# Row sums of the key softmax moved from a reduction on VectorE to a DMA transpose and products with a mask

## The chip, the cores and the metric

The kernel runs on one core of a Trainium2 chip. The time is the device time of one execution in microseconds. The engines are named as in the profile: PE (TensorE, matrix products), PEld (its weight loads), DVE (VectorE), ACT (ScalarE), POOL (GpSimd) and SP (SyncE, which here only issues DMAs). Each engine works through its own list of instructions in order and waits where it needs another's result. PSUM, where PE writes, has eight banks.

## The reference

Two independent halves are computed and set side by side in the output of shape (1, 2048, 896).

Half A is linear attention with softmax feature maps, 16 heads of 28 columns:

```python
qkv = (x @ wqkv).reshape(B, S, 3, H, Dh)            # x: 2048 x 448
pk = einsum("bhsd,hdf->bhsf", k, w_phi)             # pq likewise from q
phi_k = concatenate([softmax(pk), softmax(-pk)])    # over the 28 columns of a head
kv = einsum("bhsf,bhsd->bhfd", phi_k, v);  z = einsum("bhsf->bhf", phi_k)
o = (phi_q . kv) / (phi_q . z + 1e-6);     a = o @ wo
```

Half B is a long convolution with a state-space kernel, 448 channels with 256 states each, over 2048 positions, plus a direct term:

```python
P = exp(dt * A * l)                                 # per channel, state and position l
K = real(einsum("dn,dnl,dn->dl", C, P, dt * B))     # the kernel of each channel
y = irfft(rfft(pad(u)) * rfft(pad(K)))[:2048] + u * Dskip
```

## The kernel before

Everything works on tensors cut to 128 partitions. The SBUF is one large buffer in which the code places its tiles by hand (`sb(offset, shape)`), and PSUM is one tensor of eight banks. Each operation of the program is not issued where it is written: it is added to a list (`prog.add`), and at the end the list is issued in the order written out in `ORDER`; which banks an operation uses is written out in `SLOTS`, one entry for each `prog.take`. Nearly every instruction therefore has the line of a helper in the profile: L198 is every product, L208 a transpose on PE, L159 every DVE operation on two tensors, L171 a multiply by a number, L184 a reciprocal, L187 an activation function, L190 a copy on ACT, L213 every DMA. L592, the reduction of the key side, has a line of its own.

Half A. x is loaded in four blocks and transposed on PE (`flip_x`); w_phi is folded into the q and k weights (`fold_weights`), so that one product gives pk. The key side (`key_side`, L578 to L618) runs over 16 tiles of 128 positions. Each tile has two groups of four products of 448 columns (pk into bank b4, v into bank b5), two exponentials on ACT from pk with signs + and - into EK (128 x 2 x 448), a copy of v on ACT, the sums of EK over each head's 28 columns on DVE (`tensor_reduce`, 2 x 16 sums in f32), their reciprocal, a multiply of v (with a column of ones added) by the reciprocals into VR (128 x 2 x 29 x 16), and eight products of EK with VR that add up over all tiles in banks bK. Tiles alternate between two buffers each of EK, V, sums, reciprocals and VR. After the last tile the sums are masked by head, transposed and multiplied by wo into M. The query side (`query_side`) runs over four blocks of 512 positions.

Half B. The channels are cut into four quarters (qt). For each, sines (`rotations`) and exponentials (`dampings`) on ACT make tables which DVE multiplies together (`damp`, `far`, `hi_tables`), PE multiplies the tables into values of K at 640 positions (`build_k`), and DMAs through DRAM re-order them (`scatter_k`). `kernel_spectrum_pair` and `kernel_spectrum` transform K with products by Fourier tables (`load_f`), `signal_spectrum` does so with u early on and stores the result in DRAM (SUd), and `conv` loads it, multiplies the spectra on DVE, transforms back on PE and adds u * DSK.

Position 0 of K is not among the 640 positions. Before, a product with a matrix of ones (L349) sums the states for each channel, and L353 adds that sum to DSK on DVE, so that the direct term carries it.

Operations on two PSUM banks at once (`two`, `args`) read both with one stride; in the old `SLOTS` such pairs can lie apart, for example "07" or "26".

Of the kernel before, what the change touches and what calls it, by code (L numbers as in the profile page):

```python
# [10 lines left out]
F32 = mybir.dt.float32  # L11
# [5 lines left out]
D_MODEL = 448  # L17
# [29 lines left out]
def _dft_tables():  # L47
# [30 lines left out]
    return tuple(_round_bf16(t) for t in (G, GI, FT, pid, hm))  # L78
# [24 lines left out]
def kernel(  # L103
# [20 lines left out]
    G_d, GI_d, F_d, P_d, M_d = (nc.inline_tensor(t, name=f"const{i}").ap() for i, t in enumerate(consts))  # L124
# [96 lines left out]
    HM = sb(3200, [112, 4, D_HEAD + 1])  # L221
    bias_hp = sb(3440, [128, 1], F32)
# [122 lines left out]
    ones = sb(212544, [128, 128])  # L345
    mset(ones, 1.0)
    dma("G", DSK, bass.AP(tensor=B_Dskip.tensor, offset=B_Dskip.offset, ap=[[0, 128], [1, D_MODEL]]))
# [5 lines left out]
    add(DSK, DSK, psum[:, bs[0], 0:D_MODEL])  # L353
# [72 lines left out]
    dma("G", HM, M_d)  # L426
    dma("G", wo, A_wo.rearrange("(c p) n -> p c n", p=112))
    V_ = [sb(181504 + 928 * i, [128, D_HEAD + 1, 16]) for i in range(2)]
    for v in V_:
        mset(v[:, D_HEAD, :], 1.0)  # L430
# [147 lines left out]
    def key_side():  # L578
        bK = prog.take("P", 6), prog.take("P", 7)
        for tn in range(16):  # L580
            ts_ = slice(128 * tn, 128 * tn + 128)
            i2 = tn % 2
            (b4,), (b5,) = prog.take("P", 4), prog.take("P", 5)
            mms(acc(psum[:, b4, 0:D_MODEL], [(xT[:, dj, ts_], Wp[1][:, dj, :]) for dj in range(4)]))
            mms(acc(psum[:, b5, 0:D_MODEL], [(xT[:, dj, ts_], WV[:, dj, :]) for dj in range(4)]))
            EK = sb(177920 + 1792 * i2, [128, 2, D_MODEL])
# [3 lines left out]
            acopy(V[:, 0:D_HEAD, :], psum[:, b5, 0:D_MODEL].rearrange("p (h d) -> p d h", d=D_HEAD))  # L590
            zk = sb(187072 + 128 * i2, [128, 2, 16], F32)
            prog.add("V", lambda zk=zk, EK=EK: nc.vector.tensor_reduce(  # L592
                zk, EK.rearrange("p s (h f) -> p s h f", f=D_HEAD), axis=AX.X, op=ALU.add))
            rk = sb(187328 + 64 * i2, [128, 2, 16])
            recip(rk, zk)
            VR = sb(183360 + 1856 * i2, [128, 2, D_HEAD + 1, 16])
            mul(VR, V.unsqueeze(1).to_broadcast([128, 2, D_HEAD + 1, 16]),
                rk.unsqueeze(2).to_broadcast([128, 2, D_HEAD + 1, 16]))
            mms([(psum[0:112, bK[s][0], 116 * c:116 * c + 116].rearrange("p (d h) -> p d h", h=4),
                  EK[:, s, 112 * c:112 * c + 112], VR[:, s, :, 4 * c:4 * c + 4],  # L600
                  dict(start=(tn == 0 and c == 0), stop=(tn == 15), skip_group_check=True))
                 for s in range(2) for c in range(4)])
# [81 lines left out]
    def spectrum_terms(o, ft, b, rhs, sk0, m, cp):  # L684
        n = len(TERMS[b])
        items = [(o, ft[:, cp, fi, :], rhs(kt), dict(start=(k == 0), stop=(b == 0 and k == n - 1)))
                 for k, (fi, kt) in enumerate(TERMS[b])]
        if b == 1:
            items.append((o, (NEG, ident)[cp], sk0(1 - cp, m), dict(start=False, stop=True)))
        return items  # L690

    def kernel_spectrum_pair():
        tiles = {}

        def spec(m, b):
            (bk,) = prog.take("P", 4 + b)
            items = []
            for cp in range(2):
                items += spectrum_terms(
                    view(psum[:, bk, QC * cp:QC * cp + 1], [112, 2], [1, 112]), tiles[m], b,  # L700
                    lambda kt: view(KT[0][:, kt, 0:1], [672, 2], [1, 112]),
                    lambda c, k: view(SK[0][:, 0, c, k // 4, k % 4, 0:1], [3584, 2], [1, 112]), m, cp)
# [10 lines left out]
    def kernel_spectrum(qt, tiles, banks):  # L713
        sk = SK[qt % 2]
        for m in range(0, 8, 2):
            for b in range(2):
                (bk,) = prog.take("P", banks[b])
                items = []
                for cp in range(2):
                    for k in range(2):  # L720
                        at = 112 * (2 * cp + k)
                        items += spectrum_terms(
                            psum[:, bk, at:at + 112], tiles[m + k], b, lambda kt: KT[qt % 2][:, kt, :],
                            lambda c, i: sk[:, 0, c, i // 4, i % 4, :], m + k, cp)
# [187 lines left out]
```

## Time and profile before

| | |
|---|---|
| Median of 3 runs | 332.09 us (331.78 to 334.99) |
| The profiled execution's own time | 335.36 us |
| Its span, first to last instruction | 333.4 us |
| Instructions | 8578 |
| Busy: PE, DVE, ACT | 249.7, 267.5, 205.6 us |
| Mean granted PE clock | 0.887 |
| DMA, mean | 107 GB/s |

The span is the time from the first to the last instruction of one profiled execution. Busy time is the time in which an engine has an instruction under way; a product's end is modelled, so a busy PE need not run at its peak. The granted clock is the share of full speed that PE was allowed in a stretch. The chain of waits is found backwards from the last instruction: at each step it goes to what released it, or to the instruction before it on the same engine.

### The profile page before, as it was taken

To read this page: it belongs to the slowest core of one execution; us is meant where nothing else is said; L and a number is where in the kernel's file an instruction comes from. 1 tells how busy PE (TensorE), PEld (TensorE's weight loads), DVE (VectorE), ACT (ScalarE), POOL (GpSimd) and SP (SyncE) were. 2 spreads that over 40 slices of the span, in tenths; PEclk is the share of its full clock that TensorE was granted. 3 is DMA by queue.
4 is the path that set the end of the run, shared out by engine and by line. 5 is a ranking of instruction groups with operands and counts; after the bars stand their busy time and mean duration, and the time that the engine had idled before them with its cause. 6 is when DMAs were issued, how large, how long until landed. Compare 5 with 4: busy or idle time off the path is not lost.

```text
span 333.4 us, 8578 instructions
## 1 busy us (share of the span) xinstructions
PE 249.7 (75%) x3741; PEld 186.4 (56%) x3741; DVE 267.5 (80%) x325; ACT 205.6 (62%) x340; POOL 15.6 (5%) x31
## 2 busy tenths in 40 slices
PE   2846698896699857787967577997995608979595
PEld 2735444454355544564543375647785608879595
DVE  4286958891899988696987887999996799989990
ACT  4889548887877784866847866696544421424231
POOL 7310000000000000000010000000000000100000
PEclk9975769999999985699978989999996967979899
DMA  7999105330200000042645061787509354486022
GB/s 213 253 204 237 30 2 159 111 112 0 89 23 0 0 2 1 2 89 72 122 85 234 2 168 22 157 276 247 138 4 314 74 83 168 151 210 117 0 57 58
DMA packets 51341, 35.73 MB, mean 107 GB/s; under 512 B 32008, under 2 KB 47384, under 8 KB 50920
## 3 DMA queue, kind: packets, MB, share of 16 engines
q1 hardware_dynamic: 48328, 27.90, 34.1%
q0 software_dynamic: 2976, 7.28, 7.1%
q8 instruction: 29, 0.48, 0.6%
q14 instruction: 8, 0.07, 0.1%
HBM read 26.30 MB, written 8.85 MB: 105 GB/s over the span
## 4 chain that ended last, share of the span: by engine, by line
PE 37%; DVE 28%; DMA 15%; ACT 13%; issue 4%; SPq 2%; DVEq 0%; ACTq 0%
PE psum L198 36%; DVE sbuf L159 22%; ACT sbuf L187 7%; DMA sbuf<-in_A_x_dram 5%; DMA sbuf<-in_B_C_re_dram 4%; ACT sbuf L190 4%; DMA sbuf<-SCd 4%; DVE sbuf L592 4%; SPq L213 2%; DVE sbuf L184 1%; DMA sbuf<-const 1%; ACT L187 1%; DMA SCd<-sbuf 1%; PE psum L208 0%; DVE sbuf L177 0%
## 5 line engine op out<-in xcount | busy, mean ns | idle before, releaser
L198 PE MATMUL psum<-sbuf 128*16 128x48 bf16 (+10 forms) x3632 | 237.7, 265 | 63.3 <-ACT sbuf L187 21.5
L159 DVE TENSOR_TENSOR sbuf<-sbuf 128x896 bf16<-128x896 bf16 (+13 forms) x235 | 219.5, 975 | 32.9 <-ACT sbuf L187 16.3
L198 PEld LDWEIGHTS <-sbuf 128*16 128x16 bf16 (+4 forms) x3632 | 175.3, 112 | 125.9 <-issue 70.4
L190 ACT CAST sbuf<-psum 128x448 bf16<-128x448 f32 (+4 forms) x140 | 75.4, 570 | 77.3 <-PE psum L198 70.1
L187 ACT ACTIVATE sbuf<-psum 128x448 bf16<-128x448 f32 (+4 forms) x140 | 83.9, 659 | 33.0 <-PE psum L198 31.7
L208 PE MATMUL psum<-sbuf 128*112 128x128 bf16 (+3 forms) x109 | 13.0, 305 | 16.4 <-DMA sbuf<-in_A_x_dram 7.3
L187 ACT ACTIVATE sbuf<-psum,sbuf 128x896 bf16<-128x896 f32 (+3 forms) x28 | 21.7, 807 | 2.5 <-PE psum L198 2.1
L208 PEld LDWEIGHTS <-sbuf 128*112 128x112 bf16 (+3 forms) x109 | 11.6, 207 | 17.0 <-DMA sbuf<-in_A_x_dram 8.0
L592 DVE TENSOR_REDUCE sbuf<-sbuf 128x32 f32<-128x896 bf16 x16 | 17.2, 1080 | 1.3 <-ACT sbuf L187 1.2
L177 DVE COPY sbuf<-psum 112x1024 bf16<-112x1024 bf16 (+2 forms) x16 | 7.6, 475 | 12.8 <-PE psum L208 8.6
L187 ACT ACTIVATE sbuf<-sbuf 128x896 bf16<-128x896 bf16 (+3 forms) x13 | 11.5, 901 | 8.5 <-DVE sbuf L159 7.6
L187 ACT ACT_TABLE_LOAD x11 | 14.1, 1283 | 0.9 <-PEq L896 0.7
L171 DVE TENSOR_SCALAR sbuf<-sbuf 128x3584 bf16<-128x3584 bf16 (+4 forms) x11 | 6.7, 607 | 2.1 <-PE psum L198 1.6
L184 DVE RECIPROCAL sbuf<-sbuf 128x32 bf16<-128x32 f32 (+1 forms) x20 | 7.8, 392 | 0.6
L213 POOL DMA_DIRECT2D sbuf<-SUd x4 | 2.1, 531 | 114.2 <-DVE sbuf L159 114.2
L213 POOL DMA_DIRECT2D sbuf<-const x3 | 1.7, 569 | 114.2 <-PE psum L198 114.2
L213 POOL DMA_DIRECT2D sbuf<-in_B_u_dram x8 | 6.4, 808 | 12.2 <-PE psum L208 12.2
L159 DVE TENSOR_TENSOR sbuf<-psum,sbuf 128x128 f32<-128x128 f32 (+3 forms) x10 | 4.7, 493 | 2.0 <-ACT sbuf L187 1.3
L190 ACT COPY sbuf<-psum 112x896 bf16<-112x896 bf16 x5 | 4.3, 919 | 2.3 <-PE psum L208 2.3
L190 ACT CAST sbuf<-sbuf 128x1792 bf16<-128x1792 f32 x3 | 5.1, 1691 | 0.0
L159 DVE TENSOR_TENSOR sbuf<-sbuf,psum 112x448 bf16<-112x448 bf16 (+1 forms) x2 | 1.2, 621 | 4.3 <-issue 3.4
L174 DVE SCALAR_TENSOR_TENSOR sbuf<-sbuf 128x64 f32<-128x64 f32 (+1 forms) x6 | 3.0, 506 | 0.0
(12 smaller groups left out, 9.5 us busy)
## 6 DMA issues: line engine op xcount, KB each, us to landing
sbuf<-const SPq DMA_DIRECT2D x16, 384.0 KB, 4.2
SUd<-sbuf SPq DMA_DIRECT2D x8, 448.0 KB, 4.8
sbuf<-SCd SPq DMA_DIRECT2D x16, 224.0 KB
sbuf<-SUd POOLq DMA_DIRECT2D x4, 896.0 KB, 6.2
sbuf<-const POOLq DMA_DIRECT2D x2, 1024.0 KB, 6.0
sbuf<-in_A_x_dram SPq DMA_DIRECT2D x4, 448.0 KB, 5.1
out_dram<-sbuf SPq DMA_DIRECT2D x4, 448.0 KB
sbuf<-in_B_u_dram SPq DMA_DIRECT2D x16, 112.0 KB, 4.2
```

Of the source, the lines that this page charges most:

```text
L159: prog.add("V", lambda: nc.vector.tensor_tensor(out=o, in0=a, in1=b, op=op))
L171: prog.add("V", lambda: nc.vector.tensor_scalar_mul(o, a, s))
L174: prog.add("V", lambda: nc.vector.scalar_tensor_tensor(out=o, in0=a, scalar=s, in1=b, op0=op0, op1=op1))
L177: prog.add("V", lambda: nc.vector.tensor_copy(o, a))
L184: prog.add("V", lambda: low(lambda: nc.vector.reciprocal(o, a)))
L187: prog.add("A", lambda: nc.scalar.activation(o, a, fn, **kw))
L190: prog.add("A", lambda: nc.scalar.copy(o, a))
L198: nc.tensor.matmul(o, lhsT=l, rhs=r, **kw)
L208: nc.tensor.transpose(o, i, idn)
L213: prog.add(eng, lambda: e.dma_start(out=o, in_=i))
L592: prog.add("V", lambda zk=zk, EK=EK: nc.vector.tensor_reduce(zk, EK.rearrange("p s (h f) -> p s h f", f=D_HEAD), axis=AX.X, op=ALU.add))
```

## The change

Three things are changed together, and with them the whole of `ORDER` and `SLOTS` is written anew (1104 operations instead of 1127).

First, the key side runs over eight pairs of tiles. EK holds a pair (128 x 2 x 2 x 448). The reduction is gone: one DMA from SP transposes EK, seen as 128 x 1792, into ET, 14 blocks of 128 x 128 with the positions along the columns. For each tile of the pair seven products then take the blocks of ET as weights and a constant mask HZ (7 x 128 x 32, 1 where a row belongs to one of the 32 sums, loaded at the start) and add up 32 sums per position in a PSUM bank. One reciprocal reads the 64 sums of the pair from PSUM, and one multiply makes VR of the pair. EK, V and the reciprocals have two buffers, ET and VR one.

Second, K at position 0 becomes a term of its own. The matrix of ones holds 2^-17, its product is copied by ACT to K0 instead of added to DSK by DVE, and each spectrum of the first block of K gets, in its real part, one product more: a row block of ones with K0. DSK is loaded later.

Third, every pair of banks that one instruction reads lies in neighbouring banks in the new `SLOTS` ("12", "56", "34", "01").

```diff
@@ _dft_tables, constants @@
+    hz = np.zeros((896, 32))
+    hz[np.arange(896), np.arange(896) // D_HEAD] = 1.0
+    hz = hz.reshape(7, 128, 32).transpose(1, 0, 2)
@@ position 0 @@
-    mset(ones, 1.0)
-    dma("G", DSK, bass.AP(tensor=B_Dskip.tensor, offset=B_Dskip.offset, ap=[[0, 128], [1, D_MODEL]]))
+    mset(ones, 2.0 ** -17)
...
-    add(DSK, DSK, psum[:, bs[0], 0:D_MODEL])
+    acopy(K0, psum[:, bs[0], 0:D_MODEL])
...
     dma("G", HM, M_d)
+    dma("G", DSK, bass.AP(tensor=B_Dskip.tensor, offset=B_Dskip.offset, ap=[[0, 128], [1, D_MODEL]]))
...
+    HZ = sb(186944, [128, 7, 32])
+    dma("G", HZ, Z_d)
@@ key_side @@
-        for tn in range(16):
...
-            for s in range(2):
-                af(EK[:, s, :], psum[:, b4, 0:D_MODEL], ACT.Exp, scale=1.0 - 2.0 * s)
...
-            prog.add("V", lambda zk=zk, EK=EK: nc.vector.tensor_reduce(
-                zk, EK.rearrange("p s (h f) -> p s h f", f=D_HEAD), axis=AX.X, op=ALU.add))
-            rk = sb(187328 + 64 * i2, [128, 2, 16])
-            recip(rk, zk)
...
+        for pr in range(8):
+            i2 = pr % 2
+            EK = sb(177920 + 3584 * i2, [128, 2, 2, D_MODEL])
+            ET = sb(209216, [128, 14, 128])
+            V = V_[i2]
+            for t in range(2):
...
+                for s in range(2):
+                    af(EK[:, t, s, :], psum[:, b4, 0:D_MODEL], ACT.Exp, scale=1.0 - 2.0 * s)
+                acopy(V[:, t, 0:D_HEAD, :], psum[:, b5, 0:D_MODEL].rearrange("p (h d) -> p d h", d=D_HEAD))
+            prog.add("S", lambda ET=ET, EK=EK: nc.sync.dma_start(
+                out=ET, in_=EK.rearrange("p t s f -> p (t s f)"), transpose=True))
+            (bz,) = prog.take("P", 3)
+            mms([it for t in range(2) for it in acc(
+                psum[:, bz, 32 * t:32 * t + 32], [(ET[:, 7 * t + k, :], HZ[:, k, :]) for k in range(7)])])
+            rk = sb((187392, 138784)[i2], [128, 2, 2, 16])
+            recip(rk.rearrange("p t s h -> p (t s h)"), psum[:, bz, 0:64])
+            VR = sb(205504, [128, 2, 2, D_HEAD + 1, 16])
+            mul(VR, V.unsqueeze(2).to_broadcast([128, 2, 2, D_HEAD + 1, 16]),
+                rk.unsqueeze(3).to_broadcast([128, 2, 2, D_HEAD + 1, 16]))
...
@@ spectrum_terms @@
+        pairs = [(ft[:, cp, fi, :], rhs(kt)) for fi, kt in TERMS[b]]
         if b == 1:
-            items.append((o, (NEG, ident)[cp], sk0(1 - cp, m), dict(start=False, stop=True)))
-        return items
+            pairs.append(((NEG, ident)[cp], sk0(1 - cp, m)))
+        elif cp == 0:
+            pairs.append((W[:, 0, 31, 0:128], k0))
+        return acc(o, pairs)
@@ ORDER and SLOTS: every entry new @@
...
```

More of the change, by code (lines that the diff above doesn't have):

```diff
@@ L77, in _dft_tables @@
         hm[28 * hh:28 * hh + 28, hh, :] = 1.0
-    return tuple(_round_bf16(t) for t in (G, GI, FT, pid, hm))
+    hz = np.zeros((896, 32))
+    hz[np.arange(896), np.arange(896) // D_HEAD] = 1.0
+    hz = hz.reshape(7, 128, 32).transpose(1, 0, 2)
+    return tuple(_round_bf16(t) for t in (G, GI, FT, pid, hm, hz))
 class Prog:
@@ L123 @@
     consts = _dft_tables()
-    G_d, GI_d, F_d, P_d, M_d = (nc.inline_tensor(t, name=f"const{i}").ap() for i, t in enumerate(consts))
+    G_d, GI_d, F_d, P_d, M_d, Z_d = (nc.inline_tensor(t, name=f"const{i}").ap() for i, t in enumerate(consts))
     dram = ctx.enter_context(tc.tile_pool(name="dram", bufs=1, space=bass.MemoryType.DRAM))
@@ L221 @@
     HM = sb(3200, [112, 4, D_HEAD + 1])
+    K0 = sb(86016, [128, D_MODEL])
     bias_hp = sb(3440, [128, 1], F32)
@@ L426 @@
     dma("G", HM, M_d)
+    dma("G", DSK, bass.AP(tensor=B_Dskip.tensor, offset=B_Dskip.offset, ap=[[0, 128], [1, D_MODEL]]))
     dma("G", wo, A_wo.rearrange("(c p) n -> p c n", p=112))
-    V_ = [sb(181504 + 928 * i, [128, D_HEAD + 1, 16]) for i in range(2)]
+    V_ = [sb(o, [128, 2, D_HEAD + 1, 16]) for o in (185088, 194752)]
     for v in V_:
-        mset(v[:, D_HEAD, :], 1.0)
+        mset(v[:, :, D_HEAD, :], 1.0)
+    HZ = sb(186944, [128, 7, 32])
+    dma("G", HZ, Z_d)
     mset(W[:, 0, 31, :], 1.0)
@@ new lines, in key_side @@
+        bk_ = prog.take("P", 6, 7)
+        bK = bk_[0:1], bk_[1:2]
+        for pr in range(8):
+            i2 = pr % 2
+            EK = sb(177920 + 3584 * i2, [128, 2, 2, D_MODEL])
+            ET = sb(209216, [128, 14, 128])
+            V = V_[i2]
+            for t in range(2):
+                ts_ = slice(128 * (2 * pr + t), 128 * (2 * pr + t) + 128)
+                (b4,), (b5,) = prog.take("P", 4), prog.take("P", 5)
+                mms(acc(psum[:, b4, 0:D_MODEL], [(xT[:, dj, ts_], Wp[1][:, dj, :]) for dj in range(4)]))
+                mms(acc(psum[:, b5, 0:D_MODEL], [(xT[:, dj, ts_], WV[:, dj, :]) for dj in range(4)]))
+                for s in range(2):
[11 more added lines that the diff above has]
+                rk.unsqueeze(3).to_broadcast([128, 2, 2, D_HEAD + 1, 16]))
@@ L599, in key_side @@
             mms([(psum[0:112, bK[s][0], 116 * c:116 * c + 116].rearrange("p (d h) -> p d h", h=4),
-                  EK[:, s, 112 * c:112 * c + 112], VR[:, s, :, 4 * c:4 * c + 4],
-                  dict(start=(tn == 0 and c == 0), stop=(tn == 15), skip_group_check=True))
-                 for s in range(2) for c in range(4)])
+                  EK[:, t, s, 112 * c:112 * c + 112], VR[:, t, s, :, 4 * c:4 * c + 4],
+                  dict(start=(pr == 0 and t == 0 and c == 0), stop=(pr == 7 and t == 1), skip_group_check=True))
@@ L603, in key_side @@
+                 for t in range(2) for s in range(2) for c in range(4)])
         KVN = sb(194752, [112, 2, 4, 4, D_HEAD])
@@ L682, in load_f, with spectrum_terms @@
         return t
[L684 to L687, printed above, removed]
+    def spectrum_terms(o, ft, b, rhs, k0, sk0, m, cp):
+        pairs = [(ft[:, cp, fi, :], rhs(kt)) for fi, kt in TERMS[b]]
         if b == 1:
-            items.append((o, (NEG, ident)[cp], sk0(1 - cp, m), dict(start=False, stop=True)))
-        return items
+            pairs.append(((NEG, ident)[cp], sk0(1 - cp, m)))
+        elif cp == 0:
+            pairs.append((W[:, 0, 31, 0:128], k0))
+        return acc(o, pairs)
     def kernel_spectrum_pair():
```

17 lines of the change are left out of this document (3 added, 14 removed), and 94 rows, old and new, of tables (ORDER, SLOTS).

## The prediction

> **What bounds the kernel now.** I read the engine totals first, then cut the span into stages at the places where the chain of waits changes its colour, then the chain itself.
>
> ```profile
> span 333.4 us, 8578 instructions
> ...
> PE 249.7 (75%) x3741; PEld 186.4 (56%) x3741; DVE 267.5 (80%) x325; ACT 205.6 (62%) x340; POOL 15.6 (5%) x31
> ```
>
> DVE is the fullest engine, PE is close behind. A share of the whole span says little, so here are the stages (columns: stretch, length, busy time of PE, PEld, DVE, ACT, POOL with instruction counts, granted clock, DMA share, GB/s):
>
> ```profile
> 0.00:35.50 35.50, 19.70 (x153) 16.49 (x154) 20.27 (x21) 26.89 (x29) 11.14 (x21) 0.81 1.01 220
> 35.50:84.50 49.00, 40.41 (x255) 23.15 (x254) 34.28 (x43) 36.15 (x50) 1.20 (x4) 0.90 0.21 66
> 84.50:121.50 37.00, 31.60 (x222) 18.88 (x221) 34.88 (x41) 29.51 (x56) 0.00 (x0) 1.00 0.08 26
> 121.50:157.50 36.00, 26.25 (x581) 19.03 (x580) 27.37 (x47) 23.98 (x36) 0.00 (x0) 0.76 0.16 38
> 157.50:215.60 58.10, 44.58 (x682) 29.77 (x683) 49.08 (x55) 39.15 (x67) 1.11 (x2) 0.91 0.45 112
> 215.60:296.30 80.70, 57.64 (x1303) 49.97 (x1300) 73.46 (x90) 38.79 (x84) 2.12 (x4) 0.88 0.58 170
> 296.30:324.80 28.50, 24.96 (x464) 24.64 (x464) 28.14 (x32) 9.58 (x18) 0.00 (x0) 0.93 0.33 59
> 324.80:333.40 8.60, 4.61 (x94) 4.44 (x91) 0.00 (x0) 1.60 (x3) 0.00 (x0) 1.00 0.26 56
> ```
>
> DVE's idle time is length less busy: 15.2 us while inputs load, 14.7 up to 84.5, 2.1 in the stage to 121.5 (most of the key side), then 8.6, 9.0, 7.2 and 0.4, and 8.6 after its last instruction: 65.8 in all. From 35.5 to 324.8 it works 247.2 of 289.3 us. The chain of waits shows what the full stage is made of (start, length, what):
>
> ```profile
> 94.44 1.01 DVE sbuf L592
> 95.47 0.36 DVE sbuf L184
> 95.93 0.64 DVE sbuf L159
> 96.57 1.01 DVE sbuf L592
> ```
>
> That is one key tile: row sums (L592), reciprocal (L184), multiply (L597, through the helper L159), and the next tile 2.13 us later (96.57 - 94.44). Nothing else is waited for. At the end DVE works through without a gap, to 324.78, and 8.6 us remain after it (the last products on PE, their copies, the stores):
>
> ```profile
> 296.28 28.50 DVE L159 TENSOR_TENSOR sbuf<-sbuf 128x3584 bf16<-128x3584 bf16 x32 [0.96 <-ACT sbuf L190]
> 300.83 9.78 PE L198 MATMUL psum<-sbuf 128*128 128x112 bf16 x192 [0.16 <-DVE sbuf L159]
> ```
>
> So the time is the DVE's work, plus its 65.8 us of idle time: 267.5 + 65.8 = 333.3.
>
> **The change part by part.** The groups of instructions, by shape (busy us, mean ns of one):
>
> ```profile
> L592 DVE TENSOR_REDUCE sbuf<-sbuf 128x32 f32<-128x896 bf16 x16 | 17.2, 1080 | 1.3 <-ACT sbuf L187 1.2
> L184 DVE RECIPROCAL sbuf<-sbuf 128x32 bf16<-128x32 f32 x16 | 5.6, 352 | 0.5
> L184 DVE RECIPROCAL sbuf<-sbuf 128x64 f32<-128x64 f32 x4 | 2.2, 553 | 0.1
> L159 DVE TENSOR_TENSOR sbuf<-sbuf 128x928 bf16<-128x928 bf16 x16 | 10.3, 642 | 3.6 <-ACT sbuf L190 1.6 <-issue 0.6
> L159 DVE TENSOR_TENSOR sbuf<-sbuf 128x1792 bf16<-128x1792 bf16 x36 | 38.3, 1088 | 1.0 <-ACT sbuf L190 0.6
> L159 DVE TENSOR_TENSOR sbuf<-sbuf,psum 128x448 bf16<-128x448 bf16 x1 | 0.6, 621 | 3.4 <-issue 3.4
> ```
>
> *DVE.* Out go 16 tiles at 2.13 us = 34.1. In come, for each of 8 pairs, one reciprocal of 64 elements out of PSUM into bf16 (between 0.352 and 0.553; I take 0.45, the middle), one multiply of 1856 elements (1.088 x 1856 / 1792 = 1.13) and the 0.06 by which the step of 2.13 exceeds its three instructions (1.080 + 0.352 + 0.642 = 2.07): 1.64, eight times 13.1. The add of L353 (0.62), which also waited 3.4 us, goes to ACT as a copy. Together 34.1 + 0.6 - 13.1 = 21.6 us less DVE work; by the two reciprocal bounds 20.8 to 22.4.
>
> ```profile
> L198 PEld LDWEIGHTS <-sbuf 128*128 128x128 bf16 x1176 | 82.3, 105 | 38.5 <-issue 26.0 <-DMA sbuf<-const 1.2
> L198 PE MATMUL psum<-sbuf 128*128 128x112 bf16 x808 | 47.3, 226 | 11.8 <-ACT sbuf L187 5.8 <-DVE sbuf L159 3.5 <-issue 2.0
> L190 ACT CAST sbuf<-psum 128x448 bf16<-128x448 f32 x64 | 33.4, 538 | 42.0 <-PE psum L198 35.1 <-DVE sbuf L159 4.5 <-issue 1.8
> L187 ACT ACT_TABLE_LOAD x11 | 14.1, 1283 | 0.9 <-PEq L896 0.7
> ```
>
> *PE.* In come 8 x 14 = 112 products that load 128x128 weights and stream 32 columns. No row has that shape. Back to back, products with such weights and 112 columns take 9.78 / 192 = 0.051; their mean with all starts and stalls is 0.226. So 5.7 to 25.3 us; I take 0.105, the mean weight load, since 14 at a time make a short run: 11.8. Position zero adds 8 products of 224 columns and 16 of 112: 24 x 0.051 = 1.2, at most 24 x 0.226 = 5.4; I take 2. PE goes from 249.7 to 263.5, its part after 35.5 us from 230.0 to 243.8. That is nearly DVE's old 247.2, and this is what limits the gain.
>
> *ACT.* The same 32 exponentials and 16 copies of the key side, one copy more (0.54), and, reading the new ORDER by the number of each operation, 13 changes of function table between exponential and sine where the old one has 11: 2 x 1.283. So 3.1 us more on an engine that is idle for 127.8: nothing, unless it falls in the stage up to 84.5, where 36.15 of 49 are busy.
>
> *The DMA transposes.* SP issues eight, each moving 128 x 1792 x 2 bytes = 448 KB inside SBUF, and waits first for the pair's four exponentials. Behind them on SP stand stores of SUd, read much later; x rows and signal rows for the second half stand ahead of the first. PE now waits for each landing before its 14 sums, with later key products and signal products queued behind; DVE waits for the sums before its reciprocal, with damp and table work behind. The landing has only neighbours in the trace (KB each, median us from issue to landing):
>
> ```profile
> SUd<-sbuf SPq DMA_DIRECT2D x8, 448.0 KB, 4.8
> ...
> sbuf<-in_A_x_dram SPq DMA_DIRECT2D x4, 448.0 KB, 5.1
> ...
> sbuf<-in_A_wqkv_dram SPq DMA_DIRECT2D x1, 392.0 KB
> ...
> sbuf<-in_B_B_re_dram SPq DMA_DIRECT2D x1, 224.0 KB, 18.4
> ...
> SCd<-sbuf SPq DMA_DIRECT2D x4, 32.0 KB, 3.2
> ```
>
> I take 4.8, the same bytes out of SBUF in the same stage; the ends are 3.2 and 18.4. As there is one ET buffer, a pair's period is landing plus sums, 4.8 + 14 x 0.105 = 6.3. The room for it: the first key exponentials run at 42.2, and the last pair's sums stand in PE's new list ahead of all K products of table 0, which before waited for the end of the table work at 133.7.
>
> ```profile
> 42.23 1.00 ACT L187 ACTIVATE sbuf<-psum 128x448 bf16<-128x448 f32 x2
> 129.65 4.08 DVE L159 TENSOR_TENSOR sbuf<-sbuf 128x896 bf16<-128x896 bf16 x6
> ```
>
> With four exponentials the first transpose can go at 44.2; if 133.7 moves 12 us forward, to 121.3, there are 77.1 us for eight, 9.6 each, so landings up to 9.6 - 1.5 = 8.1 are hidden. At 4.8 there is cover.
>
> [...] No transpose is in this trace.
>
> *The front.* The last B or C row lands at 35.5 and starts the chain:
>
> ```profile
> 4.71 16.11 DMA sbuf<-in_A_x_dram
> 20.83 14.66 DMA sbuf<-in_B_C_re_dram
> 35.52 1.29 DVE sbuf L159 x2
> ```
>
> In the new SP list one block of x (448 KB) and WV (392 KB) come after these rows: 840 KB at 220 GB/s = 3.9 us earlier. But PE's new list has the first signal products and one more flip ahead of CR. Between 0 and 3.9 I take 2, and set it against the table loads and first landing: net 0.
>
> *The bank pairs and the new order.* No row separates the two-bank instructions by their pair, so I give them no price. What may go is PE's waiting for ACT:
>
> ```profile
> PE psum L198 <- ACT sbuf L187: 21.5, 17, 4.8
> ...
> PE psum L198 <- ACT sbuf L190: 15.6, 18, 2.3
> ```
>
> That is 37.1 us of an engine that mostly isn't last; I book nothing and keep it as the way to the low end.
>
> **The sum.** If DVE stays the wall with its idle time unchanged, 21.6 us go. If PE becomes the wall with the idle time DVE had, the wall falls from 247.2 to 243.8: 3.4 go. The key stage says that both bite: DVE's 34.88 of 37 would shrink by more than a third, but PE has 31.60 there and gets sums on top, so the freed DVE time must be filled with table work drawn forward, which the new list does. I take the middle, 12.5. Span 333.4 - 12.5 = 320.9. The profiled execution took 335.36 with 1.96 around its span, so 322.9; the median of the three runs lies 3.3 below it, at 332.09, so 332.1 - 12.5 = 319.6: **320 us**.
>
> **The rivals.** *Full relief*: the list fills every hole and the freed DVE time counts whole: 332.1 - 21.6 = 310. For it: DVE is the fullest engine in every stage from 84.5 to 324.8. Against: PE at 85% of the stage. *PE takes over*: 332.1 - 3.4 = 329. For it: the 31.60 of 37. Against: PE's granted clock is 0.76 and 0.81 in two stages, so some of its busy time can shrink. *Slow transposes*, the other side: above a landing of 8.1 each further microsecond is paid eight times, since one ET buffer lets nothing overlap; at 8.1 + 12.5 / 8 = 9.7 the gain is gone. Halfway between 4.8 and 18.4, at 11.6, it costs 8 x 3.5 = 28: 348 us. For it: PE's list has the sums of pairs 3 and 4 six groups apart, DVE's has only a copy between pairs 3 and 4; against: the 448 KB row. *The relief does not show*, since new waits take it: 332.
>
> Chances: the forecast 0.52 (its own range 313 to 328), full relief 0.10, PE takes over 0.16, no relief 0.07, slow transposes 0.15. A measurement of this kernel tells about 1% from no change, 328.8 to 335.4. Faster: 0.52 + 0.10 and half of PE takes over, 0.70. Same: the other half and most of no relief, 0.14. Slower 0.16. For 8 in 10 the range leaves out most of the slow transposes and half of full relief: 309 to 338.
>
> **What would show it.** Right: no reduce, DVE busy near 246, PE near 263, transposes landing near 5 us, and damp of table 0 running among the key pairs. PE takes over shows as DVE idle behind PE between pairs; slow transposes as PE waiting on a DMA into SBUF eight times, growing. Wrong would also be a DVE total that fell with a span that did not.

## The result and the profile after

The changed kernel took 301.82 us (median of 4 runs, 300.59 to 303.41), the kernel before, timed beside it, 333.54 (331.78 to 343.97). The ratio is 0.907, 95% interval 0.899 to 0.915: 31.7 us gained, where 12.5 were forecast, and below the low end of the range. Some executions take longer than others of the same kernel (343.97 us against 331.78, 3.7%, for the kernel before); the ratios here and below leave these out.

The span and the engine totals of the changed kernel:

```profile
span 299.6 us, 8829 instructions
...
PE 240.7 (80%) x3877; PEld 179.8 (60%) x3877; DVE 244.4 (82%) x292; ACT 203.4 (68%) x343; POOL 16.0 (5%) x32
```

DVE's work fell by 23.1 us (267.5 to 244.4) and its idle time by 10.7 (65.9 to 55.2): together the 33.8 us that the span lost. PE executes 136 more products and is busy 9.0 us *less*, at a mean granted clock of 0.949 after 0.887. Neither the idle time nor PE's fall stood in the forecast.

The stages, cut where the prediction cut the old kernel as far as 215.60 (columns as there: stretch, length, PE, PEld, DVE, ACT, POOL, granted clock, DMA share, GB/s):

```profile
0.00:35.50 35.50, 16.46 (x120) 12.21 (x121) 19.82 (x24) 24.11 (x26) 10.36 (x19) 1.00 0.89 191
35.50:84.50 49.00, 39.18 (x355) 24.63 (x353) 26.71 (x33) 44.59 (x72) 2.51 (x7) 0.98 0.61 125
84.50:121.50 37.00, 35.88 (x448) 24.03 (x452) 34.15 (x39) 30.83 (x52) 0.00 (x0) 0.93 0.27 63
121.50:157.50 36.00, 29.88 (x451) 18.69 (x443) 32.37 (x38) 26.98 (x43) 0.00 (x0) 0.91 0.26 65
157.50:215.60 58.10, 45.93 (x1086) 34.88 (x1087) 55.18 (x69) 41.40 (x67) 1.24 (x3) 0.85 0.53 136
215.60:292.00 76.40, 69.63 (x1357) 61.78 (x1355) 75.29 (x92) 34.45 (x85) 1.94 (x4) 1.00 0.65 177
```

Two things show. In the second stretch ACT is now busy for 44.59 of 49 us (36.15 before) and DVE for only 26.71: five of the eight key pairs sit there, and DVE has less to do than the stage lasts. From 121.50 on DVE is idle for 7.7 us up to 292.00, where it was idle for 25.2 up to 324.8: the long middle of the kernel has closed up.

The groups of the parts that the prediction priced (busy us, mean ns of one, idle time before them):

```profile
L201 PE MATMUL psum<-sbuf 128*128 128x32 bf16 x112 | 4.1, 178 | 6.2 <-DMA sbuf<-sbuf 3.3 <-DMA sbuf<-const 2.9
L187 DVE RECIPROCAL sbuf<-psum 128x64 bf16<-128x64 f32 x8 | 4.4, 555 | 19.4 <-PE psum L201 19.4
L162 DVE TENSOR_TENSOR sbuf<-sbuf 128x1856 bf16<-128x1856 bf16 x8 | 9.0, 1120 | 2.7 <-ACT sbuf L193 1.4 <-PE psum L201 1.1
```

And what waits (total us, times, longest), in the order of the answer:

```profile
DVE sbuf L187 <- PE psum L201: 19.4, 5, 8.4
...
PE psum L201 <- ACT sbuf L190: 6.6, 7, 2.5
...
PE psum L201 <- ACT sbuf L193: 5.1, 10, 1.0
...
PE psum L201 <- DMA sbuf<-sbuf: 3.3, 1, 3.3
```

PE's waiting for ACT went from 37.1 to 11.7 us. DVE has a new wait, 19.4 us, for the sums that PE now makes. The landing itself, from the DMA issues between 40 and 120 us (KB each, median us to landing, of those whose landing the view could assign):

```profile
SUd<-sbuf SPq DMA_DIRECT2D x5, 448.0 KB, 4.5
...
sbuf<-in_A_wo_dram POOLq DMA_DIRECT2D x1, 392.0 KB, 10.0
sbuf<-sbuf SPq DMA_TRANSPOSE x8, 3.9
```

The 3.9 is that of one transpose, the last. In this trace the semaphore of each of the eight transposes rises 16 times between its issue and the next issue on that semaphore, and the last rise is taken as its landing. Read so, seven of the eight transposes landed in 3.9 to 4.6 us, and that of pair 4 (the pairs are counted from 0), issued at 74.23, in 10.35.

### The profile page after: what moved, and what is told of

Its sections match the earlier page's. It is cut to its first block, busy times and chain, and to the rows that moved or that the text cites. A ratio compares the mean times of both kernels' runs of the same rounds, so it can differ in the third digit from the quotient of the medians.

```text
span 299.6 us, 8829 instructions
## 1 busy us (share of the span) xinstructions
PE 240.7 (80%) x3877; PEld 179.8 (60%) x3877; DVE 244.4 (82%) x292; ACT 203.4 (68%) x343; POOL 16.0 (5%) x32
## 5 line engine op out<-in xcount | busy, mean ns | idle before, releaser
L201 PE MATMUL psum<-sbuf 128*16 128x48 bf16 (+9 forms) x3768 | 231.3, 258 | 39.1 <-DVE sbuf L162 11.1
L201 PEld LDWEIGHTS <-sbuf 128*16 128x16 bf16 (+4 forms) x3768 | 170.7, 109 | 98.3 <-issue 37.3
L162 DVE TENSOR_TENSOR sbuf<-sbuf 128x896 bf16<-128x896 bf16 (+13 forms) x227 | 216.7, 1002 | 12.1 <-DMA sbuf<-SCd 3.5
L190 ACT ACTIVATE sbuf<-psum 128x448 bf16<-128x448 f32 (+4 forms) x140 | 81.7, 674 | 13.2 <-DVE sbuf L162 7.5
L211 PE MATMUL psum<-sbuf 128*112 128x128 bf16 (+3 forms) x109 | 11.7, 267 | 16.2 <-DMA sbuf<-in_A_x_dram 7.2
L190 ACT ACTIVATE sbuf<-psum,sbuf 128x896 bf16<-128x896 f32 (+3 forms) x28 | 21.7, 812 | 0.0
L211 PEld LDWEIGHTS <-sbuf 128*112 128x112 bf16 (+3 forms) x109 | 10.0, 172 | 17.8 <-DMA sbuf<-in_A_x_dram 7.7
L187 DVE RECIPROCAL sbuf<-psum 128x64 bf16<-128x64 f32 x8 | 4.4, 555 | 19.4 <-PE psum L201 19.4
L190 ACT ACTIVATE sbuf<-sbuf 128x896 bf16<-128x896 bf16 (+3 forms) x13 | 11.6, 915 | 3.6 <-DVE sbuf L162 3.4
L180 DVE COPY sbuf<-sbuf 128x448 bf16<-128x448 bf16 (+1 forms) x6 | 1.4, 238 | 3.1 <-DMA sbuf<-const 3.1
L196 POOL MEMSET sbuf<- 128x32 bf16 (+3 forms) x6 | 1.4, 261 | 24.7 <-PE psum L211 24.5
```

Of the source, the lines that this page charges most:

```text
L162: prog.add("V", lambda: nc.vector.tensor_tensor(out=o, in0=a, in1=b, op=op))
L180: prog.add("V", lambda: nc.vector.tensor_copy(o, a))
L187: prog.add("V", lambda: low(lambda: nc.vector.reciprocal(o, a)))
L190: prog.add("A", lambda: nc.scalar.activation(o, a, fn, **kw))
L196: prog.add("G", lambda: nc.gpsimd.memset(o, v))
L201: nc.tensor.matmul(o, lhsT=l, rhs=r, **kw)
```

## The experiments

Each profiled execution is read as DVE's work plus DVE's idle time, which add up to its span. All ratios are to the kernel before, timed beside it.

| Kernel | Ratio (95%) | Span | DVE work | DVE idle | PE waits for ACT |
|---|---|---|---|---|---|
| before | 1 | 333.4 | 267.5 | 65.9 | 37.1 |
| old kernel, far reads split | 0.938 (0.933-0.942) | 312.8 | 266.0 | 46.8 | 8.0 |
| old kernel, pairs in neighbouring banks | 0.955 (0.946-0.964) | 313.4 | 266.1 | 47.3 | 11.7 |
| changed, sums by reduction | 0.914 (0.905-0.923) | 305.7 | 260.3 | 45.4 | 15.5 |
| changed | 0.907 (0.899-0.915) | 299.6 | 244.4 | 55.2 | 11.7 |
| changed, once more | 0.913 (0.908-0.918) | 301.5 | 244.5 | 57.0 | 11.5 |
| changed, pairs apart | 1.059 (1.051-1.067) | 352.2 | 245.4 | 106.8 | 53.5 |
| changed, pairs apart, far reads split | 0.904 (0.898-0.910) | 299.3 | 245.0 | 54.3 | 12.0 |
| changed, no sums | 0.894 (0.888-0.900) | 297.8 | 244.7 | 53.1 | 11.9 |
| changed, output weights later | 0.897 (0.891-0.903) | 297.9 | 244.7 | 53.2 | 11.5 |

(PE's waits for ACT are the sums of the rows of products on L187 and L190 of the old line numbers, without those of PE's transposes; the helpers' lines move by a few from kernel to kernel. The profiled execution of the reduction is the longest of its four runs, 1.6 us over their median, and that of the old kernel with neighbouring pairs the shortest of its four, 1.4 under.)

**Sums by reduction.** The new order, banks and pairs, but the sums by one reduction on DVE for each pair; no transposes and no mask products.

```diff
-            prog.add("S", lambda ET=ET, EK=EK: nc.sync.dma_start(
-                out=ET, in_=EK.rearrange("p t s f -> p (t s f)"), transpose=True))
...
-            mms([it for t in range(2) for it in acc(psum[:, bz, ...], [(ET[...], HZ[...]) for k in range(7)])])
+            prog.add("V", lambda zk=zk, EK=EK: nc.vector.tensor_reduce(
+                zk, EK.rearrange("p t s (h f) -> p (t s h) f", f=D_HEAD), axis=AX.X, op=ALU.add))
...
-            recip(rk..., psum[:, bz, 0:64])
+            recip(rk..., zk)
```

> The changed kernel and its order of work, but each pair's 64 sums come from one reduction on VectorE (128 x 1792 into 64 sums) at the place where the products with the mask stood; no transpose, no such products. Theory 'VectorE's work counts whole': eight reductions of about 2.1 us each come back, 17 us, so 302 + 17 = 319 us. Rival 'the order made the gain': in the key stage VectorE waits 19.4 us for the sums anyhow, the reductions fill that time, and the kernel stays between 302 and 309 us; then the new order is worth over 24 of the 32 us, and the sums under 7.

Measured: 306.31 us (303.33 to 307.91), 0.914. Nearly the whole gain is there without the transposes, as the rival had it. The totals of its page:

```profile
span 305.7 us, 8591 instructions
...
PE 240.2 (79%) x3765; PEld 178.1 (58%) x3765; DVE 260.3 (85%) x300; ACT 204.9 (67%) x343; POOL 16.1 (5%) x32
```

The sums by transpose take 15.9 us from DVE (260.3 to 244.4). The span falls by 6.1 only, because DVE's idle time grows by 9.8. The medians differ by 4.5 us and the ratios by 0.007, or 2.3 us, and the intervals overlap: a gain of the sums in themselves isn't shown clear of the noise.

**Pairs apart.** The changed kernel with each PSUM bank given another number, so that pairs that were neighbours lie three or four banks apart. Which tiles share a bank, the order and the work stay.

```diff
-        return SLOTS[len(self.jobs) - 1] if SLOTS else slots
+        got = SLOTS[len(self.jobs) - 1] if SLOTS else slots
+        return sorted((0, 4, 1, 5, 2, 6, 3, 7)[c] for c in got) if kind == "P" else got
```

> The changed kernel with its eight PSUM banks renamed (0 to 0, 1 to 4, 2 to 1, 3 to 5, 4 to 2, 5 to 6, 6 to 3, 7 to 7), so that who shares a bank with whom stays as it is, but every two-bank tile lies three or four banks apart. Theory 'neighbouring banks matter': TensorE's waits for ScalarE go from 11.7 back towards the 37.1 us of before, and the time to 308 us or more. Rival 'only the names change': 302 us, within 1%.

Measured: 353.95 us (351.54 to 355.75), 1.059: 52 us lost by bank numbers alone, and slower than the kernel before. Its totals and waits, and what one read of two banks takes:

```profile
span 352.2 us, 8827 instructions
...
PE 257.2 (73%) x3877; PEld 185.3 (53%) x3877; DVE 245.4 (70%) x292; ACT 208.1 (59%) x343; POOL 16.0 (5%) x32
```

```profile
PE psum L202 <- ACT sbuf L191: 31.9, 32, 3.9
...
PE psum L202 <- ACT sbuf L194: 21.6, 28, 2.3
```

```profile
L191 ACT ACTIVATE sbuf<-psum 128x896 bf16<-128x896 f32 x36 | 32.2, 920 | 17.6 <-PE psum L202 17.3 <-DVE sbuf L181 0.3
```

In the changed kernel, with the same 36 reads from neighbouring banks:

```profile
L190 ACT ACTIVATE sbuf<-psum 128x896 bf16<-128x896 f32 x36 | 32.4, 949 | 0.2 <-PE psum L201 0.2
```

The read itself isn't slower (920 ns against 949). What grew is waiting. In the compiled programs of these kernels a waiting instruction names the semaphore count, and so the instruction, that it waits for. Compared by the banks that both touch, the changed kernel has no wait between two instructions without a bank in common that meet only in a bank *between* the two of a read; this one has 89, of them 51 of PE on ACT. The kernel before has 54, of them 23 of PE on ACT. So a read of banks 0 and 4 was taken, when the waits were made, for one that touches 1, 2 and 3 too. The next runs test whether these waits carry the loss.

**Mirror.** The same edit with (7, 6, 5, 4, 3, 2, 1, 0): other numbers, neighbours stay neighbours.

> The changed kernel with every PSUM bank c renamed to 7 - c and nothing else. Neighbours stay neighbours, so no read of two banks has a bank between them. The theory that distance decides (a read of two banks holds up work in the banks between them): as the changed kernel, 302 us, between 299 and 305, PE's waits for ACT again near 12 us. The rival that a renaming as such, or which bank holds what, makes the loss seen with the banks apart: 310 or more.

Measured: 301.28 us (299.16 to 304.06), 0.905. A renaming as such costs nothing.

**Far reads split, pairs apart.** The kernel of 354 us, and each access of two banks that aren't neighbours issued as two of one bank each.

```diff
+    def each(fn, *vs):
+        if not any(apart(v) for v in vs):     # first stride beyond one bank, two steps
+            return fn(*vs)
+        for i in range(2):
+            fn(*(bass.AP(tensor=v.tensor, offset=v.offset + i * v.ap[1][0],
+                         ap=[list(v.ap[0])] + [list(d) for d in v.ap[2:]]) for v in vs))
...
-        prog.add("A", lambda: nc.scalar.activation(o, a, fn, **kw))
+        prog.add("A", lambda: each(lambda o, a: nc.scalar.activation(o, a, fn, **kw), o, a))
...
-        prog.add("A", lambda: nc.scalar.copy(o, a))
+        prog.add("A", lambda: each(nc.scalar.copy, o, a))
```

> The changed kernel with the banks apart, as in the earlier run of 354 us, but each read of two banks that aren't neighbours is issued as two reads of one bank: 88 instructions of ScalarE become 176, with 0.17 us more for each pair (two of 0.54 to 0.556 for one of 0.91 to 0.92), some 15 us of ScalarE in all. No waiting pair of instructions has only a bank in between in common any more (51 waits of PE on ScalarE had). If these waits made the loss: the time comes back to 302 plus what of the 15 us shows in the stretches where ScalarE is full, 304 to 318, and PE's waits for ScalarE fall from 53.5 to under 20. If the distance costs in another way (the banks that tiles come to lie in, the reuse of banks, the width of a read): 335 to 365.

Measured: 301.29 us (300.52 to 305.18), 0.904, just below the range of the first theory. The distance as such costs nothing that shows; with the waits gone, the whole loss is gone. The totals and the rows of waits (PE's products on L212; ACT's activation functions on L201, its copies on L167 and, where they are split, on L169):

```profile
PE 241.5 (81%) x3877; PEld 180.3 (60%) x3877; DVE 245.0 (82%) x294; ACT 209.9 (70%) x431; POOL 16.0 (5%) x32
```

```profile
PE psum L212 <- ACT sbuf L201: 6.1, 6, 2.5
...
PE psum L212 <- ACT sbuf L167: 4.7, 8, 1.0
...
PE psum L212 <- ACT sbuf L169: 1.2, 3, 0.6
```

The 88 additional instructions brought 6.5 us of ACT work against the 15 expected, and none of it shows in the time.

**The old kernel with neighbouring pairs.** Only the list of banks is new; the order, the reduction and the work are the old ones.

```diff
 SLOTS = [[int(c) for c in i] for i in (
-    "0 12 34 0 26 34 6 0 4 3 7 0 7 0 7 0 6 5 07 07 26 34 02 34 02 67 34 67 7 0 34 26 02 02 23 67 17 23 17 17 23 "
+    "1 23 45 0 67 45 0 0 5 4 0 1 1 0 1 0 6 7 01 01 67 45 67 45 67 01 45 01 0 1 45 67 67 67 56 01 12 56 12 12 56 "
...
```

> The kernel before, its order, row sums and work as they were, and only the list of PSUM banks written anew: all 44 tiles of two banks now lie in neighbouring banks (before: 54 waits stand between instructions that touch no common bank, only a bank between the two of a read; here: none). The theory that the bank pairs carry the gain by themselves, whatever the order: the sums made 4.5 of it, so 304 to 310, PE's waits for ACT down from 37.1 to about 12. A middle theory, that the gain needs both the pairs and an order packed around them: DVE's idle time before its last instruction falls by a third, 314 to 322. The rival that the new order carries the gain, and that pairs apart hurt only a tight order: 328 to 335.

Measured: 316.75 us (315.37 to 318.29), 0.955, in the middle theory's range. Its totals, the waits and two stretches, the second of them the two middle stages of the prediction in one:

```profile
PE 240.0 (77%) x3741; PEld 181.1 (58%) x3741; DVE 266.1 (85%) x325; ACT 204.5 (65%) x340; POOL 15.6 (5%) x31
```

```profile
PE psum L198 <- ACT sbuf L190: 9.4, 11, 2.3
PE psum L198 <- ACT sbuf L187: 2.3, 3, 1.4
```

```profile
35.50:84.50 49.00, 43.94 (x302) 25.72 (x302) 42.78 (x49) 46.20 (x65) 1.20 (x4) 0.98 0.32 90
121.50:215.60 94.10, 77.51 (x1330) 53.52 (x1329) 86.63 (x109) 70.39 (x125) 1.65 (x3) 0.92 0.48 131
```

With the work unchanged, DVE is busy for 42.78 us of the first stretch's 49 (34.28 before) and for 86.63 of the second's 94.1 (27.37 + 49.08 = 76.45 before). That is 18.7 us more work done in the same 143.1, and the span fell by 20.0. PE's busy time fell from 249.7 to 240.0 with the very same 3741 products, at a mean granted clock of 0.918 after 0.887: the old 249.7 was no measure of its work alone.

**The old kernel with its far reads split.** The run above moved every tile to another bank; this one keeps the old banks and only splits the 50 reads of ACT whose banks aren't neighbours, by the edit shown above.

> The kernel before, its order, its sums and its banks as they are, and only the 50 reads of ScalarE whose two banks aren't neighbours issued as two reads of one bank each, some 0.17 us more for each, 8.5 us of ScalarE in all. None of the 54 waits that had only a bank in between in common is left. If those waits made the gain of the run with the neighbouring banks (317 us, 0.955): 315 to 322, PE's waits for ScalarE from 37.1 down to about 15. If it was the new list of banks in other ways (which bank is used again when): 328 or more.

Measured: 314.02 us (311.82 to 317.43), 0.938, a little below the first theory's range: 21 us gained by adding 50 instructions. The rows of waits for ACT on the products:

```profile
PE psum L208 <- ACT sbuf L163: 4.7, 6, 2.3
...
PE psum L208 <- ACT sbuf L165: 3.0, 5, 1.2
```

With 0.3 us on a third line that is 8.0, where it was 37.1. So it was the waits on banks in between, in the old kernel too. Splitting does a little better than the new bank list by the ratios, while the two profiled spans lie 0.6 us apart (312.8 and 313.4); why stays open. In the kernel before, a read of 128 x 448 takes 538 to 558 ns and one of 128 x 896 takes 920 to 927, so the first bank of a split read may be done with earlier; no run separates that.

**Sums left out.** The changed kernel without transposes and mask products; the reciprocals read 64 of the exponentials, so the key weights aren't normalised and the result of half A is another one. The lists and the other work stay.

> The changed kernel without the transposes and without the products with the mask; the reciprocals read 64 exponentials instead of the sums, so the key weights are left unnormalised. Theory 'the waits of VectorE for the sums (19.4 us) are on the path': 302 - 10 to 15 = 287 to 292 us. Rival 'ScalarE paces the key stage (35.6 of 40 us busy between 40 and 80)': the waits only change their name, 297 to 302 us.

Measured: 298.14 us (297.76 to 299.96), 0.894. The sums in their new form, at whatever cost to PE, SP and the waits, can be had back for 4 to 6 us at most (0.894 against 0.907 and 0.913). And the wait that replaced DVE's 19.4 us:

```profile
DVE sbuf L162 <- ACT sbuf L193: 14.5, 6, 5.8
...
DVE sbuf L180 <- PE psum L211: 11.8, 6, 4.4
```

DVE, no longer held by the sums, waits for ACT's copies of v and for PE's transposes of x instead (5.2 and 6.6 us in the changed kernel), with nearly the same idle time (53.1 against 55.2). Without the sums ACT is busy for 48.04 us of the 49 from 35.5 to 84.5, so it is the limit behind them; with the sums it has 44.59.

**Landing twice.** Each transpose issued twice.

```diff
+            def turn_twice(ET=ET, EK=EK):
+                for _ in range(2):
+                    nc.sync.dma_start(out=ET, in_=EK.rearrange("p t s f -> p (t s f)"), transpose=True)
-            prog.add("S", lambda ET=ET, EK=EK: nc.sync.dma_start(...))
+            prog.add("S", turn_twice)
```

> The changed kernel with each DMA transpose issued twice into the same tile, so that a landing of 3.9 us becomes about 7.8. Theory 'there is cover up to a landing of 8.1': 302 to 306 us. Rival 'the one transposed tile makes every microsecond count eight times': 302 + 8 x 3.9 = 333 us. In between, the number of the eight that show tells how many lie on the path.

Measured: 314.56 us (311.01 to 317.47), 0.932 (0.923 to 0.941), between the two theories: by the ratios 6 to 8 us more than the two runs of the changed kernel. PE now waits for the landings 7 times:

```profile
PE psum L201 <- DMA sbuf<-sbuf: 14.0, 7, 3.4
```

The second transpose of a pair is issued only when the first has landed, and the two together take 7.9 to 10.8 us, 30 us more over the eight pairs. A fifth to a quarter of that shows. The cover is real, but it doesn't hold landings of that length.

**An earlier mask.** In the changed kernel the load of HZ stands behind the matrix of 2^-17, whose address it takes. Here that matrix lies elsewhere and HZ is loaded first.

```diff
-    ones = sb(186944, [128, 128])
+    ones = sb(212544, [128, 128])
 ORDER: the load of HZ goes ahead of the memset of ones
```

> The changed kernel with the mask HZ loaded earlier: the tile of 2 to the power -17 goes to an address of its own and the load goes ahead of it on POOL. The first pair's sums then wait for the landing of the transpose alone. If VectorE's idle time is lost time wherever it lies, the 4.7 us that its reciprocal waited go: 297 to 299. If ScalarE paces the stage (19.3 of 20 us busy from 60 to 80), nothing goes: 301 to 303.

Measured: 304.97 us (301.00 to 308.85), 0.913 (0.903 to 0.923): nothing gained. But the first pair's reciprocal still waits:

```profile
55.53 0.56 DVE L187 RECIPROCAL sbuf<-psum 128x64 bf16<-128x64 f32 x1 [4.08 <-PE psum L201]
```

It waited 4.70 in the changed kernel, where PE stood 2.90 us for the mask; here PE stands 2.48 us for the transpose, which was issued at 49.67 and not at 42.85. So the wait only changed its cause, and this run can't tell what its removal would bring.

**Filling the waits.** The early mask, and six instructions of the first high table ahead of the waiting reciprocals.

> As the run with the early mask, and six instructions of the high table of the first quarter go ahead of the reciprocals that wait (two of 0.62 us ahead of pair 1's, one of 2.02 ahead of pair 2's, one of 2.02 and two of 1.08 ahead of pair 3's), 7.4 us in all, into VectorE's idle time of the key stage. If VectorE is the wall after the key stage, the 4.2 us taken out of the later stage go as well: 292 to 297. If ScalarE paces the key stage and what follows waits for it: 299 to 303. If the late reciprocals hold up the products and the exponentials' buffers: 303 to 308.

Measured: 307.08 us (304.61 to 311.14), 0.921 (0.913 to 0.930): no gain, in the range of the third theory. DVE's idle time is 57.9 us, as in the changed kernel run once more (57.0). From 60 to 84 us, first in the changed kernel and then in this one (columns as in the stages):

```profile
60.00:84.00 24.00, 17.66 (x183) 11.85 (x179) 9.84 (x12) 23.30 (x38) 1.25 (x3) 0.97 0.60 114
```

```profile
60.00:84.00 24.00, 16.90 (x167) 11.64 (x166) 11.73 (x12) 17.58 (x30) 1.26 (x3) 0.91 0.54 103
```

The reciprocals of pairs 2 and 3 come at 71.43 and 82.75 us and not at 67.88 and 74.53, and ACT, full in this stretch before, is busy for 17.58 of 24 us. PE's products wait for these two reciprocals (2.46 and 4.26 us), and ACT waits for PE. So work put into DVE's waits here isn't free: it delays the reciprocals, and with them PE and ACT.

**The term for position zero undone.** K0 is added to the skip row by DVE, late; the 24 products are left out.

```diff
-    mset(ones, 2.0 ** -17)
+    mset(ones, 1.0)
...
-        elif cp == 0:
-            pairs.append((W[:, 0, 31, 0:128], k0))
...
+        prog.add("V", lambda: nc.vector.tensor_tensor(out=DSK, in0=DSK, in1=K0, op=ALU.add))
```

> The changed kernel with the term for position zero undone: K0 is added to the skip row by one VectorE instruction of 448 elements (0.62 us) ahead of the first multiply of the second high table, and the 24 products of the spectrum that carried it are left out. The prediction put them at 2 us of PE, 1.2 to 5.4. If the place of this add at the front, not its work, was what the change moved: the same time within 1.5 us. If the 24 products stood on the path: 1 to 4 us less. If the add on VectorE, which has no idle time after 100 us, stands on the path: 0.6 more.

Measured: 302.74 us (300.45 to 303.96), 0.909 (0.904 to 0.914), against 0.913 (0.908 to 0.918) of the unchanged one timed beside it. No difference that can be measured; PE is busy for 240.7 us with 24 products fewer, 242.0 in the unchanged one.

**The changed kernel once more**, as the measure for that run and the next.

> The changed kernel once more, unchanged, to be compared with the two runs of this call that differ from it by little: 302, within 299 to 305 by every theory. Where it stands to them on the same chip decides their sign.

Measured: 303.92 us (302.56 to 304.68).

**The output weights later.** In the changed kernel one landing is long. From its timeline (start, length, instruction, idle time before and what ended it):

```profile
74.23 1.54 SPq L600 DMA_TRANSPOSE sbuf<-sbuf  x1
74.38 0.75 POOL L216 DMA_DIRECT2D sbuf<-in_A_wo_dram  x1 [0.15 <-issue]
...
80.44 0.93 PE L201 MATMUL psum<-sbuf 128*128 128x224 bf16 x8 [1.05 <-ACT sbuf L190]
...
84.62 7.37 PE L201 MATMUL psum<-sbuf 128*128 128x32 bf16 x50 [3.26 <-DMA sbuf<-sbuf]
...
85.22 0.56 DVE L187 RECIPROCAL sbuf<-psum 128x64 bf16<-128x64 f32 x1 [8.38 <-PE psum L201]
...
91.27 0.91 ACT L193 CAST sbuf<-psum 128x896 bf16<-128x896 f32 x1 [5.19 <-PE psum L201]
```

PE's sums of pair 4 begin at 84.62, 10.4 us after the issue, and the 392 KB of the output weights, which are read only when the key side is done, travel beside the transpose. In this run they are issued by ACT some 8 us later.

```diff
-    dma("G", wo, A_wo.rearrange("(c p) n -> p c n", p=112))
+    dma("AD", wo, A_wo.rearrange("(c p) n -> p c n", p=112))
 ORDER: this load goes behind the damping exponentials of the first quarter
```

> The changed kernel with the load of the output weights (392 KB) issued from ScalarE's queue behind the damping exponentials at 86 us, where the DMA engines stand still, and not from POOL at 74.4 us beside the transpose of pair 4. In the changed kernel that transpose was issued at 74.2 and its sums began at 84.6, with PE 2.8 of 8 us busy from 76 to 84 and VectorE waiting 8.4 us for the sums. If the load beside it is what makes this landing long: pair 4's sums begin by 79 to 80, and if that stretch is on the path the time falls by 3 to 5.5 us, to 296.5 to 299. If ScalarE, 7.7 of 8 us busy in that stretch, paces it anyway: within 1.5 us of the changed kernel in the same call. If the landing is long for another reason, its sums still begin after 83.

Measured: 299.81 us (295.57 to 302.44), 0.897 (0.891 to 0.903), 4.1 us below the changed kernel timed beside it. That is under 2%, but the two intervals lie apart. It is the lowest median of the kernels that compute the whole, though its interval overlaps that of the split reads. Its rows:

```profile
81.12 5.42 PE L201 MATMUL psum<-sbuf 128*128 128x224 bf16 x54 [1.05 <-ACT sbuf L190]
...
82.09 0.40 ACTq L216 DMA_DIRECT2D sbuf<-in_A_wo_dram  x1
82.43 0.56 DVE L187 RECIPROCAL sbuf<-psum 128x64 bf16<-128x64 f32 x1 [4.90 <-PE psum L201]
```

The load beside it was the whole cause of the long landing: here the transpose of pair 4, issued at 74.92, lands in 3.94 us by its semaphore, at 78.86, where it takes 9.7 to 10.4 in all eight profiles in which the weights are loaded beside a single transpose. The sums still don't begin by 79 to 80, as expected, because in PE's list they stand behind eight products of 224 columns, which wait for ACT until 81.12 in this run (80.44 in the changed kernel) and take 0.93. The sums follow them without another wait; PE waits for no DMA between 74 and 84 us. So DVE's wait for pair 4 falls from 8.38 to 4.90, and the reciprocal comes 2.8 us earlier, not 5. The stretch behind it, first in the changed kernel and then in this one (columns as in the stages):

```profile
84.00:92.00 8.00, 7.37 (x50) 4.34 (x51) 5.57 (x4) 2.79 (x4) 0.00 (x0) 0.66 0.00 0
```

```profile
84.00:92.00 8.00, 7.73 (x59) 4.51 (x58) 6.79 (x5) 7.98 (x13) 0.00 (x0) 1.00 0.48 133
```

ACT had stood still for 5.2 of the 8 us, waiting for PE (5.19 by its row above), and now is busy throughout. PE's granted clock in these 8 us was 0.66, after its wait of 3.26 us, and is 1.00 here; how much of the 4.1 us is the clock and how much the landing itself, no run separates.

## Why the prediction was wrong

**The step that failed: "The bank pairs and the new order. No row separates the two-bank instructions by their pair, so I give them no price", and with it "I book nothing".** This was the largest part of the gain. In the old kernel the pairs alone are worth 15 to 21 us (ratios of 0.955 and 0.938), with the sums, the order and the work unchanged. The new order, the pairs of tiles and K0 together bring some 10 more by the medians (316.75 to 306.31); no run takes them apart. The row named there was the right one: PE's 37.1 us of waiting for ACT became 11.7. The reason given for not booking it, that PE "mostly isn't last", failed: DVE, which was last, stood behind those products, and its idle time fell by 18.6 us. Durations couldn't show the price, but the program could: 54 of its waits join instructions that share no bank.

**DVE's work**: forecast 21.6 us less, 20.8 to 22.4, measured 23.1. The new instructions took 0.555 and 1.120 us where 0.45 and 1.13 were put, 13.4 for all against 13.1. Some 1.4 of the 23.1 had nothing to do with them: with neighbouring banks alone DVE's busy time fell from 267.5 to 266.1. Right in the main.

**How much of it counts**: the prediction took half, since PE would become the wall. For the sums that was too much, and the wall was another. They take 15.9 us from DVE, and the time falls by 2 to 4.5 us, against the same kernel with the reduction, and even that is within the noise. The engine behind DVE is ACT, in the stretch that the prediction had marked for it ("unless it falls in the stage up to 84.5"): 44.59 of 49 us, 48.04 without the sums, while PE has 39.18. ACT doesn't pace this stretch alone. The filled waits and the load beside pair 4 show that late sums leave ACT standing, for 5.2 us in the second case. That ACT is the limit where the sums come in time rests on its busy share and on the run without sums, which gained 4 to 6 us and not the 10 to 15 of a DVE held by its waits.

**PE**: forecast 263.5 us, measured 240.7. The 112 sums took 4.1 us in all, 0.037 each, below the lower bound of 5.7; 0.105 each (11.8) was too large by almost three times. The 24 products for position zero show 1.3 us of PE's busy time and nothing in the time; 2 were booked. And the base of the sum, 249.7, held stalls and a lower clock (0.887): with neighbouring banks the same products take 240.0 at 0.918. "PE takes over", with a chance of 0.16, rested on this.

**The landing**: forecast 4.8, measured 3.9 to 4.6 for seven of eight. The 4.8 was itself the landing of one store, the only one of the eight that the view could assign; by their semaphores the other seven of the kernel before took 2.7 to 3.2 us. In the changed kernel the plain 448 KB stores out of SBUF take 2.7 to 5.6 us by theirs, and the quickest transposes 3.9; a transpose held SP for 1.54 us in the row above. The cover of 8.1 us was, if anything, too generous: landings doubled, to 7.9 to 10.8, cost 6 to 8 us. One landing of ten microseconds was there, pair 4's, and it was worth up to 4.

**The front**: net 0 forecast. DVE is idle for 15.7 us up to 35.5, 15.2 before. Right. **ACT**: 3.1 us more forecast, 2.2 less measured (205.6 to 203.4), although the 13 table loads came as read from the list.

**The rivals.** Full relief (310) came nearest, but not by its mechanism: the freed DVE time didn't count whole, another gain came on top. Slow transposes didn't happen, but for one landing of eight, pair 4's 10.35, beyond the 9.7 at which the prediction saw the gain used up.

## What to carry to other kernels

When an instruction reads two PSUM banks with one stride, look at which banks lie between them, and count in the program the waits between instructions that share no bank: here such reads held up work on the banks in between (54 such waits in the kernel before), and putting the pairs next to each other, or splitting the read in two, gave half to two thirds of what the whole change gave (15 and 21 us of 31.7). A wait of an engine that isn't last can't be booked at nothing before one has asked who stands behind the thing that waits. An engine's busy total need not be a floor: here PE's fell by 9.7 us (249.7 to 240.0) with not one product less. And a load that nobody needs soon should not be issued beside a transfer that several engines wait for: here such a transfer landed in 10.35 us with the load beside it and in 3.94 without.

## What the runs showed of the hardware

A read by ACT of two banks takes much the same time whether they are neighbours or three to four apart (949 and 920 ns for 128 x 896). A transpose of 448 KB from SBUF to SBUF landed in 3.9 to 4.6 us in seven of eight cases of the changed kernel, within the 2.7 to 5.6 that plain stores of that size took in the same trace. The one that was followed by a load of 392 KB 0.15 us later took 10.35, and the load 10.0; with the load issued 7 us after the transpose, they took 3.94 and 3.8. Fourteen products of 32 columns with a full weight load each cost PE 0.5 us for a pair of tiles (4.1 us for the 112 of eight pairs).
